# Attention of the first two pairs with all q and k ahead of v, first gates among its states (retention + gated FFN, one core)

## Chip, cores, metric

One core of a Trainium2 chip. The metric is the device time of one execution in microseconds (us). The kernel before takes 337.31 us (median of three runs, 337.24 to 337.34; a fourth, taken beside the change, 337.52).

## The reference

```python
# q, k, v: (8 batches, 8 heads, 576, 64);  w_gate, w_val: (512, 1536);  w_out: (1536, 512)
scores = (1 / sqrt(64)) * q @ k.T
gamma  = 1 - 2 ** (-5 - head)
Dmat   = where(rel >= 0, gamma ** rel, 0)           # rel = query position - key position
attn   = (scores * Dmat) @ v                        # retention: no softmax
x      = attn.transpose(0, 2, 1, 3).reshape(4608, 512)
out    = (sigmoid(x @ w_gate) * (x @ w_val)) @ w_out
```

Retention can be done in chunks of 128 positions: each chunk has scores and v products of its own ("intra"), and takes the earlier chunks through a 64x64 state for each head ("st" products build it, "inter" products apply it).

## The kernel before

The schedule is by hand: the order in the program is the order on each engine. All loads go through SyncE's one queue into a ring of buffers; an issue waits for the load eight before it. The first chunks come in "pairs" (two chunks of one batch, TensorE transposes). After the first 512 tokens a steady part follows, in steps: Pool casts k and q into `qk_nat`, SyncE issues a transposing DMA into a tile T, and TensorE takes T for the scores. Cuts are marked with `...`.

The loads, in order of issue:

```python
for A in range(2):                       # pairs 0 and 1: k g0, q g0, k g1, q g1, v g0, v g1
    for _ in load_pair(A):
        pass
load_w(0, 2); load_w(2, 2); load_w(4, 4); load_w(8, 4)     # w_gate and w_val of feature blocks 0 to 11
pair_2 = load_pair(2)
for n_wo, n_pair in ((2, 4), (6, 2), (4, 0)):              # w_out and the third pair, mixed
    ...
```

The front (all that runs before the first gates): idle products fill TensorE's waits for loads; the granted clock is 1.00 over these first 19.6 us.

```python
def fill(n):
    ps = ffn_psum.tile([P, 512], FP32, tag="ffn", ...)
    for i in range(n):
        nc.tensor.matmul(ps, lhsT=blank[:, 0:P], rhs=blank, ...)       # 512 columns
fill(10)
...
pair_qk(0, 1, QK)
pair_intra(0, 0, 0); pair_intra(0, 0, 1)
pair_st(0, 0)
tile_sv(0, 0, (on_act, on_act))          # state out of PSUM, by two ACT copies
cast_pair("q", 1, 0, nc.vector); cast_pair("q", 1, 1, nc.vector)
...
pair_inter(1, 1)
pair_out(1, 1, None)                     # xT of the fourth chunk
...
units = h_both((0, 1))                   # gate and value products of feature blocks 0 and 1, 512 columns
step(units, 1)
pair_st(1, 1)
tile_sv(1, 1, (on_act, on_act))
step(units, 3)
```

Later places that the argument needs:

```python
for t in vbd[0:2]: nc.gpsimd.memset(t, 0.0)
cast_wo(0, on_pool)
cast_pair("k", 2, 0, nc.gpsimd)          # the third pair's k (numbered 2), on Pool
...
cast_wo(11, on_pool)                     # the last weight to land
...
store(opps[0], 0, on_dve)
opps.append(ffn_psum.tile([P, 512], FP32, tag="ffn", name="op_0_3"))   # waits for that store's copy
...
for t in vbd[2:4]:
    nc.gpsimd.memset(t, 0.0)             # Pool, directly ahead of the steps' casts
casts_to(1)                              # cast_k, cast_q of step 0 on Pool, then SyncE's transposing DMA
```

## Time and profile before

| | before |
|---|---|
| span in the profile | 335.4 us |
| TensorE (PE) busy | 328.0 us, 98% |
| DMA share, first 19.6 us | 0.99 |
| first h products (feature blocks 0, 1) | 19.60 us |
| next group of h products (blocks 2, 3) | 23.52 us |

The lines behind this are in the prediction. One more view, TensorE's timeline of the kernel before (start, busy us, engine, line, operation, out<-in, shape; in brackets the idle time ahead and what ended it), is the measure of the front. The text below takes the start of the first `hg` line for "the gates start" and the second line here for "blocks 2, 3 start":

```profile
19.60 1.02 PE L610 MATMUL hg<-xT,wg_sb 128*128 128x512 bf16 x4 [0.61 <-DVE xT L389]
...
23.52 1.89 PE L610 MATMUL hg<-xT,wg_sb 128*128 128x512 bf16 x8
```

### The profile page before, as it was taken

How to read it: one execution, taken by the hardware profiler on the slowest of the kernel's cores; microseconds unless marked ns; L12 is line 12 of the kernel's file. 1: busy time of each engine (PE TensorE's matmuls, PEld its weight loads, DVE VectorE, ACT ScalarE, POOL GpSimd, SP SyncE). 2: the span in 40 equal slices, each digit the busy share in tenths (PEclk: the TensorE clock that was granted, in tenths of full speed). 3: DMA queues.
4: the chain of work that ended last, by engine and by line, in shares of the span. 5: the costliest groups of instructions: out<-in, count | busy, mean ns of one | idle time of the engine just before them, and what ended most of it. 6: DMA issues, size and time to landing. Idle time of an engine off the chain costs nothing.

```text
span 335.4 us, 7396 instructions
## 1 busy us (share of the span) xinstructions
PE 328.0 (98%) x2784; PEld 184.3 (55%) x2784; DVE 164.2 (49%) x328; ACT 167.8 (50%) x345; POOL 185.2 (55%) x327
## 2 busy tenths in 40 slices
PE   7999999999999999999999999999999999999996
PEld 3544445969666566556566555445555455444443
DVE  5744755726376356436346635542574156503320
ACT  6545635637565456355456655445646455233321
POOL 5655679779868798882448966582577500000000
PEclk9999999999999999999999999999999999999999
DMA  7999996799999999999976999499773850020002
GB/s 210 313 372 359 335 255 131 139 225 201 174 214 193 186 205 211 214 247 214 225 132 125 185 240 199 106 232 247 136 135 82 254 203 2 0 95 33 0 31 96
DMA packets 164100, 60.00 MB, mean 179 GB/s; under 512 B 144480, under 2 KB 156000, under 8 KB 164064
## 3 DMA queue, kind: packets, MB, share of 16 engines
q1 hardware_dynamic: 163920, 59.39, 83.2%
q8 instruction: 22, 0.36, 0.5%
q10 hardware_dynamic: 144, 0.13, 0.1%
q14 instruction: 14, 0.11, 0.1%
HBM read 37.75 MB, written 9.44 MB: 141 GB/s over the span
## 4 chain that ended last, share of the span: by engine, by line
PE 94%; DMA 2%; DVE 1%; SPq 1%; issue 1%; ACT 0%; POOL 0%
PE h L495 49%; PE op L561 24%; PE op L745 3%; PE hg L610 3%; PE hv L610 3%; PE pv L420 2%; PE qk L399 2%; PE pv L418 2%; DMA k32p<-in_k_dram 2%; PE st L432 2%; SPq L114 1%; PE op L551 1%; PE pvp L370 1%; PE idle L159 1%; PE st L345 0%
## 5 line engine op out<-in xcount | busy, mean ns | idle before, releaser
L495 PE MATMUL h<-xT,wg_sb 128*128 128x384 bf16 (+2 forms) x480 | 102.8, 337 | 0.2 <-DVE gv L523 0.2
L495 PE MATMUL h<-xT,wv_sb 128*128 128x384 bf16 (+2 forms) x480 | 102.8, 337 | 0.0
L252 POOL TENSOR_TENSOR qk_nat<-k,ktab 64x256 bf16<-64x256 f32 x120 | 73.3, 611 | 42.9 <-PE st L432 27.5
L523 DVE TENSOR_TENSOR gv<-g,h 128x384 bf16<-128x384 bf16 (+1 forms) x96 | 59.6, 621 | 71.8 <-PE h L495 56.4
L561 PE MATMUL op<-wo_sb,gv 128*128 128x512 bf16 x372 | 85.5, 379 | 0.0
L519 ACT ACTIVATE g<-h 128x384 bf16<-128x384 f32 (+1 forms) x96 | 52.2, 544 | 64.9 <-PE h L495 58.3
L438 DVE CAST sbd<-st 64x256 bf16<-64x256 f32 x104 | 43.7, 420 | 45.1 <-PE st L432 42.9
L495 PEld LDWEIGHTS <-wg_sb 128*128 128x128 bf16 x480 | 43.7, 98 | 31.4 <-issue 0.4
L495 PEld LDWEIGHTS <-wv_sb 128*128 128x128 bf16 x480 | 44.1, 98 | 29.0 <-issue 0.4
L273 POOL CAST vbd<-v 64x256 bf16<-64x256 f32 x120 | 47.4, 395 | 15.2 <-PE pv L420 10.6
L561 PEld LDWEIGHTS <-gv 128*128 128x128 bf16 x372 | 34.4, 98 | 36.3
L538 ACT COPY ob<-op 128x512 f32<-128x512 f32 x33 | 19.3, 585 | 47.5 <-PE op L561 42.8
L283 ACT CAST vs<-v 64x256 bf16<-64x256 f32 x104 | 41.9, 403 | 1.6
L262 POOL TENSOR_TENSOR qk_nat<-q,qtab 128x512 bf16<-128x512 f32 (+1 forms) x34 | 35.4, 1041 | 2.6
L422 ACT CAST xT<-pv 128x512 bf16<-128x512 f32 (+1 forms) x34 | 18.1, 534 | 18.1 <-PE pv L420 18.0
L401 DVE TENSOR_TENSOR pt<-qk,tri 128x512 bf16<-128x512 f32 (+1 forms) x34 | 21.2, 625 | 6.1 <-PE qk L399 5.8
L420 PE MATMUL pv<-pt,vbd 128*128 128x64 bf16 x240 | 18.0, 193 | 0.0
L432 PEld LDWEIGHTS <-qk_nat 128*128 128x128 bf16 x208 | 13.2, 98 | 8.8
L420 PEld LDWEIGHTS <-vbd 128*128 128x128 bf16 x240 | 15.2, 98 | 3.5
L418 PE MATMUL pv<-T,sbd 128*128 128x64 bf16 x216 | 17.2, 193 | 0.0
L511 DVE TENSOR_TENSOR gv<-g,h 128x256 bf16<-128x256 bf16 x24 | 10.0, 420 | 13.7 <-ACT g L509 13.3
L418 PEld LDWEIGHTS <-sbd 128*128 128x128 bf16 x216 | 15.1, 98 | 2.5
(76 smaller groups left out, 232.8 us busy)
## 6 DMA issues: line engine op xcount, KB each, us to landing
out_dram<-ob SPq DMA_DIRECT2D x34, 256.0 KB, 2.8
v<-in_v_dram SPq DMA_DIRECT2D x26, 256.0 KB, 4.1
k<-in_k_dram SPq DMA_DIRECT2D x26, 256.0 KB, 4.6
q<-in_q_dram SPq DMA_DIRECT2D x26, 256.0 KB, 5.1
wg<-in_moe_w_gate_dram SPq DMA_DIRECT2D x12, 256.0 KB, 6.0
wv<-in_moe_w_val_dram SPq DMA_DIRECT2D x12, 256.0 KB, 5.8
wo<-in_moe_w_out_dram SPq DMA_DIRECT2D x12, 256.0 KB, 5.4
k32p<-in_k_dram SPq DMA_DIRECT2D x6, 256.0 KB, 5.6
```

The source lines that it names most:

```text
L252: nc.gpsimd.tensor_tensor(out=kn[half(hh), j, :, half(hh)], in0=k32[half(j), hh::2, :], in1=ktab[half(j), c, hh::2].unsqueeze(2).to_broadc ...
L262: nc.gpsimd.tensor_tensor(out=qs[0:n], in0=q32[0:n], in1=qtab[0:n, c, :].unsqueeze(2).to_broadcast([n, H, D]), op=ALU.mult)
L273: nc.gpsimd.tensor_copy(out=vb[half(hh), j, :, half(hh)], in_=v32[half(j), hh::2, :])
L283: nc.scalar.copy(out=natural["vs", s][half(hh), j], in_=loaded[s][0][half(j), hh::2, :])
L401: nc.vector.tensor_tensor(out=pt[:, :, 0:n].rearrange("p m (j t) -> p m j t", t=64), in0=qkp[:, :, 0:n].rearrange("p m (j t) -> p m j t", ...
L418: nc.tensor.matmul(pvp[:, m, half(j)], lhsT=before[:, m, :], rhs=qT[:, m, half(j)], start=True, stop=False)
L420: nc.tensor.matmul(pvp[:, m, half(j)], lhsT=vb[:, j, m, :], rhs=pt[:, m, half(j)], start=before is None, stop=True)
L438: nc.vector.tensor_copy(out=sb[half(hh), :, half(hh)], in_=st_tiles[b][half(hh)])
L495: nc.tensor.matmul(out, lhsT=w_sb[:, kc, fc * P:(fc + 1) * P], rhs=xT[:, kc, t0 + a:t0 + e], start=(kc == 0), stop=(kc == NKC - 1))
L519: nc.scalar.activation(out=g[:, 0:n], in_=h1[:, 0:n], func=AF.Sigmoid)
L523: nc.vector.tensor_tensor(out=gvs[some[0]][:, a:e], in0=g[:, 0:n], in1=h2[:, 0:n], op=ALU.mult)
L561: nc.tensor.matmul(opp, lhsT=gvs[fc][:, nb * P:(nb + 1) * P], rhs=wo_sb[:, fc, :], start=(fc == 0), stop=(fc == NFC - 1))
```

## The change

The intent: get TensorE sooner to the point from which it is full. All q and k of both pairs are loaded ahead of both v, so that all scores can be done while v is still on its way; idle products become four times shorter, so that real work that has become ready stands less long behind them; the xT copies go to VectorE, off the ACT queue that the states need; the first gates are computed in halves of 256 tokens, the first half before the last state. The fourth output tile moves to another PSUM pool. The diff, cut to its core:

```diff
-    for A in range(2):
-        for _ in load_pair(A):
-            pass
+    both = [load_pair(A) for A in range(2)]
+    for n_pair in (4, 2):
+        for one in both:
+            for _ in range(n_pair):
+                next(one)
...
-        for i in range(n):
-            nc.tensor.matmul(ps, lhsT=blank[:, 0:P], rhs=blank, start=True, stop=True)
+        for i in range(4 * n):
+            nc.tensor.matmul(idle[-1], lhsT=blank, rhs=blank, start=True, stop=True)   # 128 columns
...
     pair_intra(0, 0, 0)
+    pair_qk(1, 1, FF)                    # last scores, among the first v products
     pair_intra(0, 0, 1)
     pair_st(0, 0)
...
+    g0 = h_bank(ffn_psum, "ffn", "hg_0", 1)[:, 0]
+    h_half("g", 0, 0, g0)                # block 0, first 256 tokens
+    gate(0, 0, g0)
     pair_inter(1, 1)
-    pair_out(1, 1, None)
+    pair_out(1, 1, on_dve, on_act)
+    g1 = h_bank(ffn_psum, "ffn", "hg_1", 1)[:, 0]
+    h_half("g", 1, 0, g1)
+    gate(1, 0, g1)
-    units = h_both((0, 1))
-    step(units, 1)
     pair_st(1, 1)
     tile_sv(1, 1, (on_act, on_act))
-    step(units, 3)
+    ... # the other six halves of blocks 0 and 1
...
-    opps.append(ffn_psum.tile([P, 512], FP32, tag="ffn", name="op_0_3"))
+    opps.append(qk_psum.tile([P, 512], FP32, tag="qk", name="op_0_3"))
```

More of the change, by code (lines that the diff above doesn't have):

```diff
@@ L148, with idle_bank @@
     LEAD_CAST = 3
-    blank = consts.tile([P, 512], BF16)
+    blank = consts.tile([P, P], BF16)
     nc.vector.memset(blank, 0.0)
+    idle = []
+    def idle_bank():
+        idle.append(ffn_psum.tile([P, P], FP32, tag="ffn", name=f"idle_{len(idle)}"))
+    idle_bank()
     def fill(n):
-        ps = ffn_psum.tile([P, 512], FP32, tag="ffn", name=f"idle_{fill.at}")
-        fill.at += 1
-        for i in range(n):
-            nc.tensor.matmul(ps, lhsT=blank[:, 0:P], rhs=blank, start=True, stop=True)
-    fill.at = 0
+        for i in range(4 * n):
+            nc.tensor.matmul(idle[-1], lhsT=blank, rhs=blank, start=True, stop=True)
     fill(10)
@@ L332, in pair_qk @@
         if g == 0:
-            probs["p", A] = att_pool.tile([P, 2, M, 2, P], BF16, tag="ptp", name=f"ptp_{A}", bufs=1)
+            probs["p", A] = att_pool.tile([P, 2, M, 2, P], BF16, tag="ptp", name=f"ptp_{A}", bufs=2)
         for hh in range(2):
@@ L359, with pair_tile @@
     pair_ps = {}
+    def pair_tile(A, a, banks):
+        s = 2 * A + a
+        ps = [psum.tile([P, M // len(banks), P], FP32, tag=tag, name=f"pvp_{s}_{i}") for i, (psum, tag) in enumerate(banks)]
+        pair_ps[s] = [(ps[m * len(banks) // M], m % (M // len(banks)), M // len(banks)) for m in range(M)]
     def pair_intra(A, g, a):
         s = 2 * A + a
-        if g == 0:
-            pair_ps[s] = (tr_psum if a else pv_psum).tile([P, M, P], FP32, tag="tr" if a else "pv", name=f"pvp_{s}")
-        ps = pair_ps[s]
+        if s not in pair_ps:
+            pair_tile(A, a, [(tr_psum, "tr") if a else (pv_psum, "pv")])
         for i in range(2):
             m = 2 * g + i
+            ps, at_m, of = pair_ps[s][m]
             for r in range(2):
                 for hh in range(2):
-                    nc.tensor.matmul(ps[half(hh), m, :], lhsT=natural["v", A][half(a), r, 2 * m + hh, :],
+                    nc.tensor.matmul(ps[half(hh), at_m, :], lhsT=natural["v", A][half(a), r, 2 * m + hh, :],
                                      rhs=probs["p", A][half(a), hh, m, r, :],
-                                     start=(m == 0 and r == 0), stop=(m == M - 1 and r == 1),
+                                     start=(at_m == 0 and r == 0), stop=(at_m == of - 1 and r == 1),
                                      skip_group_check=True)
@@ L378, in pair_inter, with pair_out @@
         for m in range(M):
-            nc.tensor.matmul(pair_ps[2 * A + a][:, m, :], lhsT=state[b, c - 1, 1][:, m, :],
+            ps, at_m, of = pair_ps[2 * A + a][m]
+            nc.tensor.matmul(ps[:, at_m, :], lhsT=state[b, c - 1, 1][:, m, :],
                              rhs=turned["qp", A][:, m, a * P:(a + 1) * P],
-                             start=False, stop=(m == M - 1), skip_group_check=True)
-    def pair_out(A, a, eng):
+                             start=False, stop=(at_m == of - 1), skip_group_check=True)
+    def pair_out(A, a, *engs):
         t0 = (2 * A + a) * P
-        if eng is not None:
-            eng(out=xT[:, :, t0:t0 + P], in_=pair_ps[2 * A + a])
-            return
-        for g, half_eng in enumerate((on_dve, on_act)):
-            half_eng(out=xT[:, 2 * g:2 * g + 2, t0:t0 + P], in_=pair_ps[2 * A + a][:, 2 * g:2 * g + 2])
+        k = M // len(engs)
+        for i, eng in enumerate(engs):
+            eng(out=xT[:, i * k:(i + 1) * k, t0:t0 + P], in_=pair_ps[2 * A + a][i * k][0])
     def phase_qk(s):
@@ L622, in step @@
             next(units)
-    cast_pair("k", 0, 0, nc.gpsimd)
+    for A in range(2):
+        for g in range(2):
+            cast_pair("k", A, g, nc.gpsimd)
+    for A in range(2):
+        for g in range(2):
+            cast_pair("v", A, g, on_pool)
+    for i in range(2):
+        cast_w("g", 0, 2, i, on_pool)
+    for i in range(2):
+        cast_w("v", 0, 2, i, on_pool)
+    QK = [(qk_psum, "qk"), (qk_psum, "qk")]
+    FF = [(ffn_psum, "ffn"), (ffn_psum, "ffn")]
+    TR, PV = (tr_psum, "tr"), (pv_psum, "pv")
     cast_pair("q", 0, 0, nc.vector)
-    cast_pair("k", 0, 1, nc.gpsimd)
+    turn("k", 0, 0, *TR)
+    turn("q", 0, 0, *PV)
+    fill(3)
     cast_pair("q", 0, 1, nc.vector)
-    cast_pair("v", 0, 0, on_pool)
-    cast_pair("v", 0, 1, on_pool)
-    cast_pair("k", 1, 0, nc.gpsimd)
-    cast_pair("k", 1, 1, nc.gpsimd)
-    cast_pair("v", 1, 0, on_pool)
-    cast_pair("v", 1, 1, on_pool)
-    QK = [(qk_psum, "qk"), (qk_psum, "qk")]
-    turn("k", 0, 0)
-    turn("q", 0, 0)
-    fill(4)
-    turn("k", 0, 1)
     pair_qk(0, 0, QK)
-    turn("q", 0, 1)
+    turn("k", 0, 1, *TR)
+    fill(2)
+    turn("q", 0, 1, *PV)
     fill(3)
-    pair_qk(0, 1, QK)
+    cast_pair("q", 1, 0, nc.vector)
+    pair_qk(0, 1, FF)
+    turn("k", 1, 0, *TR)
+    turn("q", 1, 0, *PV)
+    fill(2)
+    cast_pair("q", 1, 1, nc.vector)
+    turn("k", 1, 1, *TR)
+    pair_qk(1, 0, QK)
+    fill(1)
+    turn("q", 1, 1)
+    idle_bank()
+    fill(3)
     pair_intra(0, 0, 0)
+    pair_qk(1, 1, FF)
     pair_intra(0, 0, 1)
@@ L646 @@
     tile_sv(0, 0, (on_act, on_act))
-    cast_pair("q", 1, 0, nc.vector)
-    cast_pair("q", 1, 1, nc.vector)
-    fill(2)
-    turn("k", 1, 0)
     pair_intra(0, 1, 0)
     pair_intra(0, 1, 1)
-    fill(2)
+    pair_st(0, 1)
     pair_inter(0, 1)
-    turn("q", 1, 0)
-    pair_out(0, 0, on_act)
-    pair_st(0, 1)
-    fill(1)
-    turn("k", 1, 1)
+    pair_out(0, 0, on_dve)
     pair_out(0, 1, on_dve)
-    turn("q", 1, 1)
-    pair_qk(1, 0, QK)
     tile_sv(0, 1, (on_act, on_act))
-    fill(3)
@@ L665 @@
-    pair_qk(1, 1, QK)
-    fill(1)
     pair_intra(1, 0, 0)
-    pair_inter(1, 0)
+    pair_tile(1, 1, QK)
     pair_intra(1, 0, 1)
+    pair_intra(1, 1, 0)
     pair_st(1, 0)
     tile_sv(1, 0, (on_act, on_act))
-    fill(2)
-    pair_intra(1, 1, 0)
-    pair_out(1, 0, on_act)
+    pair_inter(1, 0)
+    pair_out(1, 0, on_dve)
     pair_intra(1, 1, 1)
-    pair_inter(1, 1)
-    pair_out(1, 1, None)
-    for i in range(2):
-        cast_w("g", 0, 2, i, on_pool)
-    cast_w("v", 0, 2, 0, on_pool)
@@ L681, with h_half @@
-    cast_w("v", 0, 2, 1, on_dve)
-    units = h_both((0, 1))
-    step(units, 1)
+    gs = [g_pool.tile([P, 512], BF16, tag="g", name=f"g_0_{fc}") for fc in range(2)]
+    for fc in range(2):
+        gvs[fc] = gv_pool.tile([P, 512], BF16, tag="gv", name=f"gv_0_{fc}")
+    def h_half(what, fc, x, ps):
+        cols = slice(x * 256, x * 256 + 256)
+        for kc in range(NKC):
+            nc.tensor.matmul(ps, lhsT=(wg_sb if what == "g" else wv_sb)[:, kc, fc * P:(fc + 1) * P], rhs=xT[:, kc, cols],
+                             start=(kc == 0), stop=(kc == NKC - 1))
+        if what == "v":
+            nc.vector.tensor_tensor(out=gvs[fc][:, cols], in0=gs[fc][:, cols], in1=ps, op=ALU.mult)
@@ L685, with gate, h_bank @@
+    def gate(fc, x, ps):
+        nc.scalar.activation(out=gs[fc][:, x * 256:x * 256 + 256], in_=ps, func=AF.Sigmoid)
+    def h_bank(psum, tag, name, n):
+        return psum.tile([P, n, 256], FP32, tag=tag, name=name)
+    g0 = h_bank(ffn_psum, "ffn", "hg_0", 1)[:, 0]
+    h_half("g", 0, 0, g0)
+    gate(0, 0, g0)
+    pair_inter(1, 1)
+    pair_out(1, 1, on_dve, on_act)
+    g1 = h_bank(ffn_psum, "ffn", "hg_1", 1)[:, 0]
+    h_half("g", 1, 0, g1)
+    gate(1, 0, g1)
     pair_st(1, 1)
     tile_sv(1, 1, (on_act, on_act))
-    step(units, 3)
+    v0 = h_bank(ffn_psum, "ffn", "hv_0", 2)
@@ L688 @@
+    h_half("v", 0, 0, v0[:, 0])
+    h_half("g", 0, 1, (g2 := h_bank(qk_psum, "qk", "hg_2", 2))[:, 0])
+    h_half("g", 1, 1, g2[:, 1])
+    h_half("v", 1, 0, v0[:, 1])
+    gate(0, 1, g2[:, 0])
+    gate(1, 1, g2[:, 1])
+    for fc in range(2):
+        h_half("v", fc, 1, h_bank(ffn_psum, "ffn", f"hv_{1 + fc}", 1)[:, 0])
     for i in range(2):
```

## The prediction

> **What bounds the kernel now.** I read the chain that ended last, then the time by stretches, then the waits of TensorE, and then, for every place where TensorE takes something that another engine or a DMA made, the two times side by side. The chain first:
>
> ```profile
> PE 94%; DMA 2%; DVE 1%; SPq 1%; issue 1%; ACT 0%; POOL 0%
> ```
>
> TensorE carries the end. The time by stretches (us, then busy us of PE, PEld, DVE, ACT, POOL, granted clock, DMA share, GB/s) says where it is not full:
>
> ```profile
> 0.00:19.60 19.60, 16.12 (x249) 8.49 (x249) 12.52 (x38) 11.90 (x24) 11.48 (x24) 1.00 0.99 275
> 19.60:335.40 315.80, 311.92 (x2536) 175.79 (x2536) 151.64 (x291) 155.89 (x322) 173.69 (x304) 1.00 0.83 173
> ```
>
> The first 19.6 us are attention of the first two pairs, padded with idle products; from 19.60 on TensorE hardly pauses. The change rebuilds the first part, so the obvious reckoning is "TensorE starts its dense stretch earlier by x, the end comes earlier by x". That holds only if nothing later is pinned to a clock of its own. Two things are. The loads: in this first part the DMA share is 0.99, and it stays above 1.0 until 46 us (the loads of weights); the Pool timeline (start, us) shows Pool waiting for each of the last ones:
>
> ```profile
> 44.80 0.61 POOL L224 CAST wo_sb<-wo 128x512 bf16<-128x512 f32 x1 [0.74 <-DMA wo<-in_moe_w_out_dram]
> 46.25 0.61 POOL L224 CAST wo_sb<-wo 128x512 bf16<-128x512 f32 x1 [0.83 <-DMA wo<-in_moe_w_out_dram]
> ...
> 47.61 1.84 POOL L781 MEMSET vbd<- 128x1024 bf16 x2
> 49.53 2.65 POOL L252 TENSOR_TENSOR qk_nat<-k,ktab 64x256 bf16<-64x256 f32 x4
> 52.26 1.04 POOL L262 TENSOR_TENSOR qk_nat<-q,qtab 128x512 bf16<-128x512 f32 x1
> ```
>
> From the last weight's landing at 46.25, Pool works without a pause to 53.30, and no instruction in it waits for TensorE. Right behind it SyncE issues the transposing DMA of the first attention step of the steady part, and a third one later (SyncE's timeline, then the tile's landing time from the view of that one DMA):
>
> ```profile
> 53.33 1.55 SPq L289 DMA_TRANSPOSE T<-qk_nat  x1
> DMA to landing us min/median/max: 3.8/3.8/3.8
> 63.78 1.28 SPq L289 DMA_TRANSPOSE T<-qk_nat  x1
> DMA to landing us min/median/max: 3.6/3.6/3.6
> ```
>
> So the first T is there at 53.33 + 3.8 = 57.1, the third at 63.78 + 3.6 = 67.4. TensorE takes them here (weight loads):
>
> ```profile
> 57.51 0.38 PEld L399 LDWEIGHTS <-T 128*128 128x128 bf16 x8
> 67.52 0.26 PEld L399 LDWEIGHTS <-T 128*128 128x128 bf16 x4
> ```
>
> Slack: 0.4 us at the first, **0.14 us at the third**. No wait shows in the kernel before, because TensorE always came just after. This is the step on which my number rests.
>
> **What the skill says.** "TensorE: Matmul & The Clock Gate", Part 1: start to start 426.7/106.7 ns for 512/128 columns cold, 215.7/55.6 warm, with the warm clock after some 3.4 us of activity. The trace agrees: the first idle products' weight loads begin 0.43 us apart, and 16 products h of 512 columns take 3.45 us in the chain, 216 ns each. "DMA: Bandwidth & Descriptors", Bandwidth, puts the HBM limit of one core near 358 GB/s; the trace has 275 over the first part and 377 from 20 to 30 us, at full DMA share: the loads are at their rate, not short of issues (an issue waits for the load eight before it). Same page, Issuing engines are not separate DMA queues: all transfers share the 16 engines and interleave; so another order of the loads reorders them but does not shorten the sum. "PSUM — Partial Sum Buffer", Specifications: eight banks of 2 KiB per partition; the kernel's pools use 1+2+1+1+3 = 8, so moving a tile to another pool is the only way to a free bank.
>
> **The change part by part.**
>
> Loads: same twelve pieces, q and k of both pairs in slots 1 to 8, v in 9 to 12. In the kernel before, the consumers of slots 5 to 12 start at 8.25, 9.15, 10.08, about 11.0, 11.88, 12.74, 13.63, 14.47, and the first weight at 15.44. Slots keep their times (estimate), so the weights land as before and the last v is cast at 14.47 + 0.61 = 15.1, as before.
>
> Idle products: 28 of 512 columns become 96 of 128, the columns of 24. The first 40 take 40 x 0.107 = 4.3 us cold, as 10 x 0.427 before. The others stand in waits. No gain of their own; they keep the gaps short.
>
> Attention of two pairs: the last q piece lands at 11.0, but VectorE has two score masks (1.29) until 11.3; cast 0.69, transposes 0.40, ACT copy 0.74, last scores 0.42: about 13.6. Then the state's chain, per step products 0.44 plus two ACT copies 0.74 plus 0.05: three steps from 13.85 reach 17.5; inter products and the xT copies (0.40 + 0.42) end near 18.4. First gate half 17.1. From there TensorE has enough: eight halves of four 256-column products at 0.109 (0.44 each, 3.5 us, as the four groups of 3.45 before), inter 0.23, last state 0.37. The group of the first two feature blocks ends near 21.2 to 22, where before it ended at 23.7 (next group begins in the chain at 23.69). **Front gain 1.5 to 2.4 us.** Extra: 16 weight loads, hidden under 109 ns of product each; ACT 4 x 0.38 for 2 x 0.60, VectorE 4 x 0.42 for 2 x 0.69, both beside TensorE.
>
> Bank of the fourth output product: from the pool that must be evacuated first to the scores' pool. It removes this wait of TensorE, 0.35 us:
>
> ```profile
> 53.16 0.59 PE L745 MATMUL op<-wo_sb,gv 128*128 128x512 bf16 x2 [0.35 <-DVE ob L538]
> ```
>
> Now what becomes of it. Weights of feature blocks 4 to 7: cast by 25.3, wanted at about 24.7 + 0.65; just enough. Pair 2's first k: Pool casts it behind the last val weights and two memsets,
>
> ```profile
> 35.06 1.07 POOL L242 TENSOR_TENSOR kp<-k32p,ktab 128x512 bf16<-128x512 f32 x1
> 37.34 0.39 PE L311 MATMUL kTp<-ident,kp 128*128 128x128 bf16 x4
> ```
>
> so it ends at 36.13 whatever TensorE does, and TensorE, that came at 37.34 (weights 37.12), can come at most 1.0 to 1.2 earlier: first cap. With the 0.35 of the bank, 1.3 to 1.5 earlier at the first output block's end. TensorE then reaches the first T near 56.1 and stands until 57.1: second cap, 0.4 left. Ten us on it reaches the third T at 67.1 and waits until 67.4: **third cap, 0.14 left**. Behind it I find slack again (fourth T lands at 72.0, taken at 74.3; sixth 83.6 for 84.6), and Pool there waits for TensorE. Sum: 337.31 - 0.14 = 337.17, say 337.1.
>
> **The rivals.** (a) *The gain is carried through.* For: the chain of the kernel before names TensorE from 20 us to the end, with no wait over 0.4 us. Against: the slacks above; a wait that is hidden does not show in a chain. If Pool or the loads ran earlier too, the end would be 1.3 to 1.5 earlier: 335.8 to 336.0. (b) *The front is no faster*: VectorE, now with all scores and three of the xT copies, or the state's chain on ACT becomes its bound. For: the states are three steps in series of 1.2 us. Against: TensorE started at 19.60 before and these end by 18.5. Even then up to 1 us of lateness is partly paid by the bank's 0.35; 337.2 to 337.9. (c) *The loads shift*: another order of requests changes the rate by some per cent, the last weight lands 0.2 to 0.5 us earlier or later than 46.25, and everything pinned to it moves along: 336.7 to 337.7. For: rates differ in the trace from 275 to 377 GB/s. Against: q, k and v pieces have one size and one shape.
>
> **Range and chances.** I give the capped reckoning some 65%, (c) in either direction 20%, (a) 8%, (b) 7%. The middle is 337.1; 8 in 10 lie in 336.3 to 337.6, wider below, since the caps can yield but the gain in front is real. Two per cent would be 6.7 us: the part before the dense stretch is only 19.6 us with 15.4 of it waiting for loads, so faster 0.01, within 2% 0.97, slower 0.02.
>
> **What would show it right or wrong.** Right: h products begin near 17 to 18 instead of 19.60; new waits of TensorE for Pool's kp near 35 to 36 (about 1 us), for the DMA of T near 56 to 57 (about 1 us) and a small one near 67.2; no wait for the evacuation at 53; the last output weight's cast still starting at 46.2 +- 0.2 and the first transposing DMA issued at 53.3. Wrong: if TensorE has no wait for T although the front is over 1 us earlier, then Pool's work after 46 us moved, and (a) or (c) holds; if h begins after 19 us, (b); if the last weight lands elsewhere, (c).

## The result

The four runs of the changed kernel took 336.28 to 337.89 us, median 337.02; the ratio to the kernel before is 0.9991, 95% interval 0.9967 to 1.0015: the same. (Ratios here and below are the mean time of one kernel's fast runs over that of the other's in the same rounds, so not quite the ratio of the medians quoted.) A repeat on another chip (e5 below: 14 runs beside 38 of the kernel before) has 337.23 against 337.15, ratio 1.0000 (0.9989 to 1.0012). So the gain is zero within 0.4 us.

The front did become faster. TensorE's timeline after:

```profile
17.26 0.61 PE L700 MATMUL hg<-xT,wg_sb 128*128 128x256 bf16 x4
...
21.79 1.89 PE L621 MATMUL hg<-xT,wg_sb 128*128 128x512 bf16 x7
```

The gates start 2.34 us earlier, and blocks 2, 3, that follow the whole group, 23.52 - 21.79 = 1.73 us earlier. Where did 1.73 us go? The chain that ended last says that TensorE alone no longer carries the end:

```profile
PE 76%; DMA 10%; POOL 8%; issue 2%; SPq 1%; DVE 1%; ACT 1%; POOLq 0%; DVEq 0%
```

TensorE's products after show the places where it now stands. Columns as above:

```profile
36.15 0.40 PE L317 MATMUL kTp<-ident,kp 128*128 128x128 bf16 x4 [0.39 <-POOL kp L248]
...
39.98 0.38 PE L317 MATMUL qTp<-ident,qp 128*128 128x128 bf16 x4 [0.40 <-ACT qT L327]
...
57.08 0.41 PE L410 MATMUL qk<-T 128*128 128x64 bf16 x8 [0.43 <-DMA T<-qk_nat]
...
67.11 0.28 PE L410 MATMUL qk<-T 128*128 128x64 bf16 x4
```

The same products before:

```profile
40.60 0.39 PE L311 MATMUL qTp<-ident,qp 128*128 128x128 bf16 x4
...
57.61 0.40 PE L399 MATMUL qk<-T 128*128 128x64 bf16 x8
...
67.63 0.28 PE L399 MATMUL qk<-T 128*128 128x64 bf16 x4
...
84.57 0.40 PE L399 MATMUL qk<-T 128*128 128x64 bf16 x8
```

At the sixth T the weight load (PEld) shows the wait, and its product starts with it:

```profile
84.42 0.29 PEld L410 LDWEIGHTS <-T 128*128 128x128 bf16 x8 [0.49 <-DMA T<-qk_nat]
```

(kp and qp are the third pair's k and q as cast for TensorE; it transposes them into kTp and qTp, which ACT copies to kT and qT.) At each hand-over, take the start time of the product before minus the start time after; that is what is left of the gain there. (The weight load is a worse mark: it starts 0.1 to 0.2 us ahead of its product where TensorE isn't held up, 37.12 for 37.34 in the kernel before, and with it where it is, 36.14 for 36.15 in the changed one. Read on weight loads, what is left comes out some 0.1 to 0.2 us too small there, and the waits look longer: 0.88 for kp, 0.71 for the first T.)

| place | before | after | left | the product's wait after |
|---|---|---|---|---|
| blocks 2, 3 start | 23.52 | 21.79 | 1.73 | |
| the third pair's first kp taken | 37.34 | 36.15 | 1.19 | 0.39 |
| its last qp taken | 40.60 | 39.98 | 0.62 | 0.40 |
| first T taken | 57.61 | 57.08 | 0.53 | 0.43 |
| third T taken | 67.63 | 67.11 | 0.52 | none |
| sixth T taken | 84.57 | 84.42 | 0.15 | 0.21 |
| a later T | 93.50 | 93.37 | 0.13 | none |

Between the last qp and the first T the 0.35 us of the bank are gained, and lost again at the first T. The 0.13 stays to 287 us (weight loads at 287.34 before, 287.21 after). All this is one profiled run of each kernel; in the profiled runs of e1, e5, e6 and e7 below, which have the changed front, blocks 2, 3 start between 21.46 and 22.47, so the front's gain was 1.05 to 2.06 us in these. The first of the pinned chains, as Pool's timeline of the changed kernel shows it, stands where it stood before (46.25, 47.61, 49.53 and 52.26 there):

```profile
46.12 0.62 POOL L230 CAST wo_sb<-wo 128x512 bf16<-128x512 f32 x1 [0.86 <-DMA wo<-in_moe_w_out_dram]
...
47.48 1.84 POOL L823 MEMSET vbd<- 128x1024 bf16 x2
49.41 2.66 POOL L258 TENSOR_TENSOR qk_nat<-k,ktab 64x256 bf16<-64x256 f32 x4
52.14 1.04 POOL L268 TENSOR_TENSOR qk_nat<-q,qtab 128x512 bf16<-128x512 f32 x1
```

The last weight lands when it landed, Pool works on without a pause, and SyncE's timeline has the transposing DMA at 53.21 where it had 53.33.

### The profile page after: what moved, and what is told of

Its sections match the earlier page's. It is cut to its first block, busy times and chain, and to the rows that moved or that the text cites. A ratio compares the mean times of both kernels' runs of the same rounds, so it can differ in the third digit from the quotient of the medians.

```text
span 335.2 us, 7536 instructions
## 1 busy us (share of the span) xinstructions
PE 325.7 (97%) x2836; PEld 190.0 (57%) x2868; DVE 165.1 (49%) x331; ACT 167.6 (50%) x345; POOL 186.4 (56%) x328
## 4 chain that ended last, share of the span: by engine, by line
PE 76%; DMA 10%; POOL 8%; issue 2%; SPq 1%; DVE 1%; ACT 1%; POOLq 0%; DVEq 0%
PE h L506 42%; PE op L572 22%; DMA wo<-in_moe_w_out_dram 3%; POOL qk_nat L258 3%; PE pv L431 2%; PE qk L410 2%; DMA k32p<-in_k_dram 2%; PE pv L429 2%; DMA wv<-in_moe_w_val_dram 2%; DMA k<-in_k_dram 2%; POOL qk_nat L268 2%; PE st L443 1%; POOL vbd L279 1%; DMA T<-qk_nat 1%; SPq L114 1%
## 5 line engine op out<-in xcount | busy, mean ns | idle before, releaser
L572 PE MATMUL op<-wo_sb,gv 128*128 128x512 bf16 x356 | 84.5, 379 | 0.8
L412 DVE TENSOR_TENSOR pt<-qk,tri 128x512 bf16<-128x512 f32 (+1 forms) x34 | 21.2, 625 | 6.1 <-PE qk L410 5.8
```

Source lines behind the costliest of these rows:

```text
L412: nc.vector.tensor_tensor(out=pt[:, :, 0:n].rearrange("p m (j t) -> p m j t", t=64), in0=qkp[:, :, 0:n].rearrange("p m (j t) -> p m j t", ...
L572: nc.tensor.matmul(opp, lhsT=gvs[fc][:, nb * P:(nb + 1) * P], rhs=wo_sb[:, fc, :], start=(fc == 0), stop=(fc == NFC - 1))
```

## Experiments

The theory: the front's gain is real and is lost at hand-overs pinned to loads and to Pool, so freeing a pin alone does nothing, and freeing it along with the change gives the gain back. The rivals: the front's gain is not worth that much in the first place (the end does not follow the front), or loads and rates shifted and ate it.

Twelve kernels ran, in four lots on three chips, each beside runs of the kernel before on the same chip. All runs were classed as fast; where a few had a lower granted clock, it is said.

### e1, e2: the Pool memset moved to VectorE, in the changed kernel and in the kernel before

```diff
     for t in vbd[2:4]:
-        nc.gpsimd.memset(t, 0.0)
+        nc.vector.memset(t, 0.0)
```

The 1.84 us memset stands on the pinned chain (47.48 above). Moved away, step 0's casts and the first T come earlier.

> The changed kernel with the two clears of vbd (1.84 us of Pool at 47.5 us) moved to VectorE, nothing else. Theory (the gain of the front is held up by Pool's chain behind the last weight, which ends in the first T): the first transposing DMA is issued up to 1.0 us earlier than 53.2 (then bounded by the landing of the first k near 48.4), TensorE's wait of 0.7 us for the first T goes or nearly goes, and the time falls by 0.3 to 1.0 us below the changed kernel's 337.0, to 336.0 to 336.7, unless a later load holds it up. Rival (the front's gain is lost elsewhere, or was never there): no change, 336.9 to 337.1.

> The kernel before with the same two clears moved to VectorE. Theory: its TensorE never waits for T, so an earlier T buys nothing: first T issued up to 1.0 us earlier than 53.33, but the time within 0.15 us of 337.3. Rival (the clears cost time by themselves, whatever the front does): 0.5 to 1.0 us faster, as in the changed kernel.

Measured: e1 336.00 us (5 runs, 335.28 to 336.69), ratio 0.9968 (0.9956 to 0.9980). e2 337.16 us (13 runs), ratio 1.0003 (0.9995 to 1.0011). In e1, SyncE issues the first transposing DMA at 52.22 instead of 53.21, and TensorE takes T with no wait:

```profile
56.48 0.38 PEld L410 LDWEIGHTS <-T 128*128 128x128 bf16 x8
```

In e2 the DMA is issued at 52.22 as well, and TensorE takes T when it did before, because it is not there sooner:

```profile
57.47 0.38 PEld L399 LDWEIGHTS <-T 128*128 128x128 bf16 x8
```

So the same edit is worth nothing to the kernel before and 1.16 us to the changed one (337.16 - 336.00 compares the two kernels that both have it). The second cap of the prediction is shown.

### e3, e4: idle products added ahead of the first gates of the changed kernel

```diff
+    fill(10)        # e3: 40 products of 128 columns, some 2.2 us; e4: fill(20), some 4.4 us
     g0 = h_bank(ffn_psum, "ffn", "hg_0", 1)[:, 0]
```

> The changed kernel with 40 more idle products of 128 columns (40 x 56 ns = 2.2 us of TensorE) right ahead of the first gate products, that is 0.5 us more than the front had gained. Theory (all but 0.1 to 0.2 of the front's gain was slack): TensorE comes 1.3 us later to pair 2's first transposes (no wait left there), 0.6 us later to the first T than that lands now, and at the sixth T is about where it is held up now: 337.0 to 337.6, at most 0.6 us slower. Rival (TensorE's time carries to the end): 2.2 us slower, 339.2.

> The same with 80 more idle products (4.4 us). Theory: the slack (about 2 us) is used up and the rest carries through: 2.0 to 2.8 us slower than the changed kernel, 339.0 to 339.8, the slope between this and the 2.2 us run near one. Rival (TensorE's time carries to the end): 4.4 us slower, 341.4. Other rival (the loads bound everything up to 50 us and more): under 1 us slower.

Measured: e4 339.86 us (4 runs), ratio 1.0079 (1.0066 to 1.0092), 2.7 over the kernel before for 4.4 added. TensorE waits for nothing at the hand-overs:

```profile
60.57 0.38 PEld L410 LDWEIGHTS <-T 128*128 128x128 bf16 x8
```

The trace lets one follow the delay: blocks 2, 3 start at 27.09, 3.57 later than in the kernel before, the first T is taken 3.06 later (60.57 for 57.51), and the span is 3.0 longer (338.4 for 335.4). Of the 0.5 that is made up on the way, 0.35 is the bank's wait, which this kernel does not have. So behind blocks 2, 3 the end follows the front. By the medians 4.4 - 2.7 = 1.7 us were absorbed. This agrees with the front's 1.73 only roughly: the bank's 0.35 ought to be absorbed as well, and in the profiled run the front was itself about 1 us late (the idle products begin at 18.33, where the gates began at 17.26). e3: 337.96 us (22 runs), ratio 1.0024 (1.0011 to 1.0037), +0.8 for 2.2; but 4 of its runs had a granted clock of 0.988 to 0.995 (339.12 to 341.19 us), and the profile fell on one of them. The other 18 have a median of 337.77, +0.6, where 2.2 - 1.7 gives 0.5, or 0.1 if the bank's 0.35 is taken off too. This subset was chosen after the fact; e4 does not need it. From e3 to e4 the 2.2 us more cost 1.9 (by all runs) to 2.1 (by the 18): once the slack is used up, the end follows the added time nearly one for one.

### e9: the same on the kernel before

```diff
+    fill(10)        # 10 products of 512 columns
     units = h_both((0, 1))
```

> The kernel before with 10 idle products of 512 columns (2.16 us) ahead of its first gate products, where TensorE stood 0.6 us waiting: the gates begin about 1.55 us later. Theory: this kernel has next to no slack in that direction (TensorE came to the first and third T just after they landed), so 1.3 to 1.6 us slower: 338.5 to 338.8. Rival (the loads bind this kernel too): under 0.5 us slower.

Measured: 338.56 us (7 runs), 1.41 over the kernel before (337.15), ratio 1.0037 (1.0023 to 1.0051). The gates and the first T move by the same 1.44 us:

```profile
21.04 1.03 PE L610 MATMUL hg<-xT,wg_sb 128*128 128x512 bf16 x4
...
58.95 0.38 PEld L399 LDWEIGHTS <-T 128*128 128x128 bf16 x8
```

(Part of the 2.2 us went into the 0.61 us that TensorE stood there for xT.) So in the kernel before a later front costs one for one and an earlier one gains nothing: the end was carried by TensorE, with the nearest other chain less than half a microsecond behind. The rival "the end does not follow the front" is out.

### e5: the changed kernel again

> The changed kernel itself, once more on the chip of this group, as the level that the others are read against. Both theories: 336.7 to 337.1, 0.1 to 0.4 us under the kernel before of the same rounds; its runs spread over more than 1 us (the first four lay between 336.28 and 337.89), because its end hangs on transfers.

Measured: the figures are in the result. The waits return: the weight loads stand 1.18 us for kp, 0.71 for the first T, 0.41 for the sixth. The runs spread more than those of the kernel before (standard deviation 0.59 against 0.34 us).

### e6: the output tile's bank undone

```diff
-    opps.append(qk_psum.tile([P, 512], FP32, tag="qk", name="op_0_3"))
+    opps.append(ffn_psum.tile([P, 512], FP32, tag="ffn", name="op_0_3"))
```

> The changed kernel with the fourth output product back in the pool whose bank must be evacuated first. Theory (0.7 us of TensorE's time ahead of the first T is slack): a wait of some 0.35 us for that evacuation is back near 51.8, the wait for the first T is shorter by as much, the first T is taken at the same 57.1 (plus or minus 0.2), the time does not change (within 0.2 us of the changed kernel, as far as its spread lets one see). Rival (TensorE's time carries through): first T taken 0.35 us later, time 0.35 us longer.

Measured: 337.16 us (12 runs), ratio to the kernel before 0.9999 (0.9987 to 1.0012), as e5. TensorE's waits (line waited for, total us, times, longest) show one wait in the place of another:

```profile
PE op L787 <- DVE ob L549: 0.3, 1, 0.3
...
PE qk L410 <- DMA T<-qk_nat: 0.2, 1, 0.2
```

```profile
57.10 0.29 PEld L410 LDWEIGHTS <-T 128*128 128x128 bf16 x8 [0.47 <-DMA T<-qk_nat]
```

The evacuation wait of 0.3 is back, the weight load's wait for T shrank from 0.71 to 0.47, and T is taken at 57.10 instead of 57.08. A wait that ends before a fixed appointment is free; so removing it was worth nothing here.

### e8: the first gates whole, after the fourth chunk, as before

```diff
-    g0 = ...; h_half("g", 0, 0, g0); gate(0, 0, g0)          # and the seven other halves
     pair_inter(1, 1)
     pair_out(1, 1, on_dve, on_act)
+    units = h_both((0, 1))
+    step(units, 1)
     pair_st(1, 1)
     tile_sv(1, 1, (on_act, on_act))
+    step(units, 3)
```

> The changed kernel with the first two feature blocks computed as in the kernel before: whole groups of 512 columns after all xT copies, not halves among the state's products. Theory: the group after them begins 0.5 to 1.0 us later than 21.79, pair 2's first transposes wait that much less for Pool, the first T is taken at the same 57.1, time within 0.2 us of the changed kernel. Rival (TensorE's time carries through): 0.5 to 1.0 us slower.

Measured: 337.25 us (14 runs), ratio 1.0006 (0.9993 to 1.0019). Blocks 2, 3 start at 22.55, 0.76 later than in the changed kernel. But this run's second and third state products, which come ahead of the edit, were already 0.24 late (15.19 and 16.46 for 14.95 and 16.22). So by these two traces the half gates are worth some 0.5 of the front's 1.73 us, and the rest of the change some 1.2. Of this loss nothing is left at the first T:

```profile
57.21 0.29 PEld L410 LDWEIGHTS <-T 128*128 128x128 bf16 x8 [0.90 <-DMA T<-qk_nat]
```

### e7: e1 with the third pair's k freed too

```diff
-    for n_wo, n_pair in ((2, 4), (6, 2), (4, 0)):
+    for n_wo, n_pair in ((0, 4), (8, 2), (4, 0)):
...
+    cast_pair("k", 2, 0, nc.gpsimd); cast_pair("k", 2, 1, nc.gpsimd)
     for t in vbd[0:2]: nc.gpsimd.memset(t, 0.0)
     cast_wo(0, on_pool)
-    cast_pair("k", 2, 0, nc.gpsimd); cast_pair("k", 2, 1, nc.gpsimd)
-    cast_wo(1, on_dve)
     cast_pair("q", 2, 0, nc.vector); cast_pair("q", 2, 1, nc.vector)
+    cast_wo(1, on_dve)
```

> The changed kernel with the clears of vbd on VectorE (as in the run that did only this) and, besides, pair 2's four first pieces loaded ahead of the first two output weights, their k cast on Pool ahead of the other two clears. Theory (caps in series: Pool's k of pair 2 near 36.1, then the first T near 56.0): TensorE no longer waits for pair 2's k (taken near 35.2), but stands some 0.5 us for the first T, which still cannot land before about 56.0; time 335.7 to 336.2, within 0.3 us of what the clears alone gave (0.9968 of the kernel before). Rival (the k of pair 2 was the only thing that held TensorE): 0.8 to 1.1 us below that, near 335.0.

Measured: 336.60 us (14 runs), ratio 0.9997 (0.9977 to 1.0016). Five runs had a granted clock of 0.990 to 0.993 and took 338.42 to 339.05 us; the other nine have a median of 336.28 (again chosen after the fact). In the profiled run the front was 1.0 us late (gates at 18.27 instead of 17.26), so kp and T came without a wait, but for that reason. And TensorE stood 0.95 us at 40.65 for ACT's copy of the third pair's qT. That copy is behind a weight cast in ACT's queue; the cast waited 1.80 us for its load and began at 39.35, 0.57 later than in e1 (38.78), though that load kept its place in the order. So in this run another pinned wait stood where the freed one had been. Inconclusive: it can't be told whether the freed k moved the cap to the first T.

### e10, e11: all later pins freed, in the changed kernel and in the kernel before

Both have the edits of e7, and step 0's loads and Pool casts moved ahead of the last four output weights, whose casts go to VectorE and ACT. The part added to e7:

```diff
-    for n_wo, n_pair in ((0, 4), (8, 2), (4, 0)):
+    for n_wo, n_pair, n_step in ((0, 4, 0), (8, 2, 1), (4, 0, 0)):
...
+        for _ in range(n_step):
+            load(0)
...
-    cast_wo(8, on_act); cast_wo(9, on_pool); cast_wo(10, on_act); cast_wo(11, on_pool)
     loads_to(1)
+    casts_to(0)                          # wo8 to wo11 follow later, by turns on ACT and VectorE; the memset of qk_nat[0] moves up
```

> The one before and, besides, the first step's v, k, q loaded ahead of the last four output weights and cast by Pool ahead of them (two of these weights' casts go to VectorE), so that the first transposing DMA is issued near 48 to 49 instead of 52 to 53. Theory (the change's gain is real and was held up only by Pool's chain behind the loads): no wait for T, nor for pair 2's k; the front's 1.7 us and the bank's 0.35 us come through, less what later transfers hold up: 335.0 to 335.7. Rival (a further bound of the loads or of TensorE's own work): no better than 336.0.

> The kernel before with the same later edits (clears on VectorE, pair 2 and the first step early), without the change under study. Theory: its front is as slow as ever and TensorE never waited behind it, so 336.9 to 337.3, and the change, measured between this kernel and the one with the same edits after it, is worth 1.3 to 2.0 us. Rival (the edits are worth something by themselves): over 0.5 us faster than the kernel before, and the change worth under 1 us even here.

Measured: e10 336.12 us (10 runs), ratio 0.9971 (0.9957 to 0.9984); e11 337.35 us (22 runs), ratio 1.0007 (0.9999 to 1.0015). With the pins gone in both, the change is worth 337.35 - 336.12 = 1.23 us; with the pins in place it was worth 0.0 (e5). Both expectations were missed, though not by much: the pair was to give 1.3 to 2.0, and e10 alone 335.0 to 335.7, where its rival said "no better than 336.0" and 336.12 was measured. Of the front's 1.73 and the bank's 0.35, some 0.85 us did not reach the end, though e10's trace has no wait for T or kp after 24 us. So a further bound is not excluded. Nor is e11 free of waits: in its only trace, of its slowest run (339.03), TensorE stands 0.22 us for VectorE's cast of the third pair's q and 0.54, up to 42.74, for a product of VectorE, where the kernel before does not. Where e10's 0.85 us went stays open: the only trace of e10 is of a run whose clock fell in the front, which the windows show (us, then busy us of PE, PEld, DVE, ACT, POOL, granted clock, DMA share, GB/s):

```profile
14.00:16.00 2.00, 0.66 (x30) 0.52 (x28) 1.62 (x3) 0.70 (x2) 1.25 (x3) 1.00 1.08 337
16.00:18.00 2.00, 1.92 (x63) 1.68 (x63) 0.89 (x2) 0.94 (x4) 1.76 (x3) 0.92 1.06 325
18.00:20.00 2.00, 2.00 (x20) 1.39 (x18) 0.69 (x1) 0.66 (x3) 1.64 (x4) 0.50 1.04 354
```

TensorE was busy 0.66 of 2 us from 14 to 16, and from 18 to 20 it ran at half the clock. In the clean profiled run of the changed kernel it was busy 1.42 us in 14 to 16 and the clock held. Over all runs: kernels with the changed front and no added products (the changed kernel, e1, e5 to e8, e10) had 9 of 73 runs under a granted clock of 0.998, and e3 4 of 22. Kernels with the front of before (112 runs of the kernel before in the first three lots, and 42 of e2, e9 and e11) had none of 154. That the thinner padding around 14 to 16 us is the cause is argued from the windows, not shown. The traces fit it in so far as the two profiled runs whose clock fell, e10 and e3, are those with the least TensorE work there: 0.66 and 1.02 of 2 us, against 1.33 to 1.97 in the other eight with the changed front. But in both TensorE stood there, 0.85 and 0.78 us, for Pool's cast of the first pair's second v, which Pool began 2.37 and 2.23 us after the first v's, with its load late (0.86 to 1.74 us after it in the other eight). Less padding and v so late in the order are not told apart.

### e12: e10 with idle products around the first states

```diff
     pair_intra(0, 0, 1)
+    fill(1)
     pair_st(0, 0)
...
+    fill(2)
     pair_st(0, 1)
...
+    fill(1)
     pair_st(1, 0)
```

> The best version so far (step 0 early, on the changed kernel) with 16 more idle products of 128 columns in three waits of the front (4 ahead of the first state products, 8 ahead of the second, 4 ahead of the third), some 0.9 us of TensorE that stood idle there. Of 73 runs with the changed front 9 had a granted clock under 0.998, of 154 with the front of the kernel before none. Theory (the clock drops where TensorE idles in the front): no run under 0.998, median 335.7 to 336.2, spread smaller; front not later than 17.3 by more than 0.2 us in an undisturbed run. Rival (the drop has nothing to do with these pauses, or the products come in the way): about one run in eight still under 0.998, or the front 0.4 us later and the median 336.2 to 336.6.

Measured: 335.91 us (5 runs, 335.40 to 336.33; the kernel before beside it 337.50, 9 runs), ratio 0.9955 (0.9942 to 0.9969): the lowest median here, clear of the kernel before and of the changed one, though far under the 2% of a verdict; its interval overlaps those of e1 and e10, so that it is faster than they are is not shown. In the window 14 to 16 TensorE is busy 1.97 of 2 us. But the gates start later than the expectation allowed:

```profile
18.14 0.61 PE L705 MATMUL hg<-xT,wg_sb 128*128 128x256 bf16 x4
...
56.45 0.38 PEld L412 LDWEIGHTS <-T 128*128 128x128 bf16 x8
```

0.88 us later than 17.26, which is about the added products' own time (16 of them at some 55 ns): most of it was not hidden in waits. None of the five runs had a low clock; at the rate of 9 in 73 five clean runs in a row would come up in about half of all tries, so this is no proof that the padding cures the clock.

## Why the prediction was right

By its own steps:

- **Front gain 1.5 to 2.4 us.** Measured 1.73 at the start of blocks 2, 3; gates at 17.26, forecast "17 to 18". (Its sum is a little loose: ends at 21.2 to 22 against 23.7 are 1.7 to 2.5.) The parts fit as well: last scores done at 13.64, forecast 13.6. The first idle products took 3.83 us, not 4.3, on which nothing hung.
- **First cap, Pool's kp: 1.0 to 1.2 left, a wait of about 1 us.** Measured 1.19 left at the product, 0.98 at the weight load, on which the prediction reads its slacks. The weight load waited 0.88, the product only 0.39. That this cap alone could be freed with profit is not shown: e7, which was to free it, is inconclusive.
- **Bank: 0.35 removed.** The wait is gone, and e6 shows what it is worth at the end: nothing, as the second cap implied.
- **Second cap, the first T: 0.4 left, a wait of about 1 us.** Measured 0.53 left (0.43 by weight loads), wait 0.43 (0.71), less than forecast because the wait for qT below took its part first. e1 against e2 frees this cap: 1.16 us appear.
- **Third cap, the third T: 0.14 left. This step failed.** The prediction let the third T land at 67.4 as before. It landed earlier, since SyncE issued it at 62.91 instead of 63.78: the issue of a q load just ahead of it took 0.64 us where it had taken 1.69. (Pool's cast for that T was done at nearly the same time, 62.97 before and 62.89 after, so it was the issue that had held the T up.) TensorE took that T without a wait, 0.52 earlier. Read on products the slack would have been 67.63 - 67.4, some 0.25, and not 0.14. SyncE's timelines, before and then after:

```profile
61.98 1.69 SPq L105 DMA_DIRECT2D q<-in_q_dram  x1
63.78 1.28 SPq L289 DMA_TRANSPOSE T<-qk_nat  x1
```

```profile
61.85 0.64 SPq L105 DMA_DIRECT2D q<-in_q_dram  x1
62.91 1.25 SPq L295 DMA_TRANSPOSE T<-qk_nat  x1
...
79.58 2.71 SPq L295 DMA_TRANSPOSE T<-qk_nat  x1
```

- **"Behind it I find slack again (sixth T 83.6 for 84.6)". This failed too, and took the third cap's place.** The sixth T's issue took 2.71 us (1.80 before) and it landed after 4.8 us (4.2 before), at 84.38. TensorE, earlier by half a microsecond, waited for it (the weight load 0.49, the product 0.21) and kept 0.15; 0.13 was left after it. So the size of the sum, 0.14, came out right through another tile than the one named. In so small a term this is partly luck: which T is late depends on the length of single issues, which differ from 0.6 to 1.7 us for one and the same load.
- **Not foreseen:** TensorE waited 0.40 us at 39.98 for ACT's copy of the third pair's qT, which stood behind a weight cast that waited 1.51 us for its load. What was left fell there from 1.19 to 0.62 us, as much as at any other place. The first T, that left 0.53, decided over it; in e1, where that T is earlier, this wait is still there (0.32).
- **Rivals.** (a), the gain carried through (335.8 to 336.0), is what e1 and e12 look like, and nearly e10 (336.12), once pins are freed; without that it did not happen. (b), a front no faster, is out by 17.26. (c), loads shifted: the last weight's cast starts at 46.12 for 46.25, inside the band given; but which T was late did hang on transfers.
- **A reading of the prediction that doesn't hold:** it sets 377 GB/s beside a limit of 358 for one core and concludes that the loads are at their rate. 377 was measured, so 358 was not the bound here; the conclusion rests on the DMA share (1.03 in the same window) alone.

The median of 337.02 and the repeat's 337.23 lie on either side of the 337.1 forecast. The trace's 0.14 us cannot be told from zero by either.

## What to carry to other kernels

A chain that is 94% one engine says what carries the end, not by how much: before shortening that engine's work, list at each hand-over when the tile lands and when it is taken, and take the smallest slack for the gain. Read both on the products, not on the weight loads that run ahead of them. Then look at what pins the landing (here a weight's load and a 1.84 us memset on Pool) and free it along with the change; either edit alone was worth nothing here, both together over 1 us. And a wait that ends just ahead of such an appointment is not worth removing by itself.

## What the Trainium skill lacked or had wrong

- "TensorE: Matmul & The Clock Gate", Why this matters for your kernels, says that throughput drops are avoided with "No PE-idle gaps >~3µs". Here half clock came in the front of e10's profiled run, in which TensorE's longest pause ahead of it, after the first idle products, was 0.85 us; TensorE's busy share was low instead (0.66 of 2 us); that this was the cause is not shown. The same page's A second HAM failure mode tells of drops by frequent short idles, but for another cause and with no number for how much busy time is enough.
- Same page, Part 1, gives about 3.4 us of sustained activity to be at full clock again, in a window that runs freely. In e3's profiled run the granted clock stayed at 0.50 from 18 to 24 us with TensorE busy 2.00 of every 2 us, mostly on idle products of 128 columns.
- No page: the length of a SyncE issue of one and the same 128 KB load, 0.64 or 1.69 us, and of one and the same transposing DMA, 1.80 or 2.71 us (the sixth T's, before and after). "Perfetto Trace Analysis", DMA Instruction — HWDGE, says that the profiled window holds the wait for the lock and the making of descriptors, without figures. Here these lengths decided which T was late.
